# A banded convolution with its operands exchanged, and a transposing transfer in place of a bounce through DRAM

## The chip, the core and the metric

The kernel runs on one core of a Trainium2 chip. The metric is device time in microseconds; the kernel before takes 749.12 us (median of three runs, 748.72 to 749.59). The core has five engines that work side by side, each through its own list of instructions in order: PE (TensorE, the matrix unit; its weight loads are shown apart as PEld), ACT (ScalarE), DVE (VectorE), POOL (GpSimd) and SP (SyncE, which here only issues DMA transfers). They wait for each other through semaphores.

## The reference

```python
def _attn_ref(x, weight):                 # x (8, 4096, 192), weight (8 heads, 7 taps)
    ...
    w = softmax(weight, axis=-1)
    x_pad = zeros before the first token, 6 of them, per batch row
    x_unf = x_pad[:, idx, :].reshape(B, S, K, H, group)      # group = 24 channels per head
    out = np.einsum('hk,bskhg->bshg', w, x_unf)

def _moe_ref(x, w_in, w_out):             # 32768 tokens, 192 -> 2048 -> 192
    h = x @ w_in
    g = np.where(h > 0.0, h, np.exp(np.minimum(h, 0.0)) - 1.0)
    return (g @ w_out).astype(np.float32)
```

So each token's 24 channels of a head become a weighted sum of the last seven tokens' channels (a causal convolution, seven taps per head), and the result goes through two matrix products with an ELU between them.

## The kernel before

Tokens are handled in 32 super steps of 1024 (two groups of 512; `s` or `t` counts super steps). In a super step the 2048 hidden columns are cut into 16 blocks of 128, so there are 512 "pairs" `n = 16 s + q`. Pair `n` computes hidden block `q` for both groups. Its chain is:

1. PE, L706 (`H`): three pairs of matmuls, `w_in` stationary, `att` moving, 512 columns each. The two matmuls of a pair use the upper and the lower 64 rows of the array at the same time and write to two banks of PSUM.
2. ACT, L499: `E = exp(H)`, one instruction per group.
3. POOL, L410: clip `E` to [0, 1].
4. DVE, L561: `gT = max(E - 1, H)`, in fp16. This frees the slot of `H`.

PSUM has three slots for `H` in a ring; a pair takes the next one and waits until whoever held it before is done (`wait_slot`; for an earlier pair that is DVE's L561). The second product (L741, `ops`) takes `gT` as stationary and `w_out` as moving operand, 192 columns, again as pairs over both row halves. These matmuls fill the gaps between the pairs: the list `GAPS` says how many go after which pair. One half of a super step's output is 64 such pairs, spread over seven gaps. An entry is "turned" when its row halves write to exchanged banks; where a list goes from unturned to turned entries of the same accumulator, PE waits (`s_swap`) until its own earlier matmuls have ended. When the last entry of a half is done, ACT evacuates (L470, `osb`) and SP sends the rows out (L322).

The convolution of a coming super step is put in the same gaps, twice per super step (`CONV_AT`): after pair 2 and after pair 10, each in the middle of a gap of two lists (5 entries, then 6 turned ones). A convolution item `("c", m)` takes one slot of the ring. It works as follows (L661 to L687). `xg` holds windows of 128 tokens as rows; `Tr` holds for each head a band matrix of 128 rows with the softmaxed taps. The window's 24 channels of a head are stationary and 122 band columns move, so that the output has channels as rows and tokens as columns: 8 heads, 5 pieces, 40 matmuls, four of which run side by side in column groups of 32. ACT copies the result to `csb` (L479, one instruction of 1024 columns). SP writes it to DRAM (`conv_slots`, L773) and, when it has landed, reads it back in the order that `att` needs with three transfers (L334). In all a super step has two writes and six reads for this. In every super step the convolution after pair 2 is for group 1 of the next super step, and that after pair 10 for group 0 of the one after it.

POOL also issues the loads of `x` (L362, two per super step, after pairs 3 and 11, five and four windows), two super steps ahead. SP's list holds, in order, the bounce's transfers and the output's.

The first super step is convolved in another way (L648), and the next three convolutions (`EARLY_CONV`, after pairs 3, 6 and 10 of super step 0) write to `ops`, which is not yet in use; `warm_pair` puts matmuls on zeros between the first pairs. In the last super step there is no convolution left.

The order of PE, ACT and SP around a convolution is made by one list:

```python
for n in range(NP):
    s, i = divmod(n, NQ)
    slot_of_pair[n] = take_slot(("h", n))
    order.append(("h", n))
    gaps = list(rounds_at.get(n, ()))
    if len(gaps) == 2:
        order.append(("o", gaps.pop(0)))
    ...
    if s:
        for at, ahead, g in CONV_AT:
            if at == i and s + ahead < NS:
                conv_at(s + ahead, g)
    if gaps:
        order.append(("o", gaps[0]))
```

Of the kernel before, what the change touches and what calls it, by code (L numbers as in the profile page):

```python
# [12 lines left out]
P = 128  # L13
HP = 64
# [4 lines left out]
CPH = 24  # L19
SLOT = 32  # L20
CW = 122
ZW = 256
GS = 512
SUP = 2 * GS
PAD = KSIZE - 1
NWIN = 9
NXB = 2
# [7 lines left out]

CONV_AT = ((2, 1, 1), (10, 2, 0))
EARLY_CONV = {3: (1, 0), 6: (1, 1), 10: (2, 0)}
FREE_CONV = 3
QUAD = 4
XTW = 136  # L40
HALO = 2
XW = 5
X_AT = ((3, 1), (8, 0), (11, 2))

PIECES = (
    ((0, 0, CW, 0), (1, 0, CW, CW), (2, 0, CW, 2 * CW), (3, 0, CW, 3 * CW), (4, 0, 24, 4 * CW)),
    ((4, 24, 24, 0), (5, 0, CW, 24), (6, 0, CW, 24 + CW), (7, 0, CW, 24 + 2 * CW),
     (8, 0, CW, 24 + 3 * CW)),
)


def bass_lightweight_conv__then__act_elu_kernel(
# [35 lines left out]

    def conv_at(s, g):
        m = 2 * s + g - 2  # L90
        if m >= FREE_CONV:
            slot_of_conv[m] = take_slot(("c", m))
        order.append(("c", m))

# [37 lines left out]
# [7 lines that stand above are left out]
        if n in EARLY_CONV:  # L139
            conv_at(*EARLY_CONV[n])  # L140
        if s:
            for at, ahead, g in CONV_AT:
                if at == i and s + ahead < NS:
                    conv_at(s + ahead, g)
        if gaps:
            order.append(("o", gaps[0]))
# [36 lines left out]
    taps = nc.dram_tensor("conv_taps", (HEADS, ZW), BF16).ap()  # L183
    bounce = nc.dram_tensor("conv_slots", (2, 2, P, SUP), BF16).ap()

    with ExitStack() as stack:
        def sbuf(name, shape, dt):
            return stack.enter_context(nc.sbuf_tensor(name, shape, dt))
# [4 lines left out]
        def sema(name):  # L193
            return stack.enter_context(nc.semaphore(name))
# [12 lines left out]
        sel = sbuf("sel", [HEADS, P], BF16)  # L207
        xg = sbuf("xg", [P, NXB, NWIN, D], BF16)
        Tr = sbuf("Tr", [P, HEADS, CW], BF16)
        csb = sbuf("csb", [P, 4, 2, GS], BF16)  # L210
        att = sbuf("att", [P, 2, 3, GS], BF16)
        w_in = sbuf("w_in", [P, 3, FF], BF16)
# [16 lines left out]
        s_wp = sema("s_wp")  # L229
        s_wb = sema("s_wb")  # L230
        s_wc = sema("s_wc")
        s_id = sema("s_id")
# [21 lines left out]
        s_ce = sema("s_ce")  # L254
        s_dw = [sema(f"s_dw{i}") for i in range(4)]
        s_band = sema("s_band")
# [16 lines left out]

        NDMA_ATT = 6
        x_need, z_need = {}, {}
# [47 lines left out]

        def read_att(eng, W, s, g):

            m = 2 * s + g - 2
            W(s_dw[m % 4], 16 * (m // 4 + 1))
            for j in range(3):
                src = bass.AP(
                    tensor=bounce.tensor,  # L330
                    offset=(2 * P * (s % 2) + j) * SUP + GS * g,
                    ap=[[SLOT * SUP, HEADS], [3 * SUP, 8], [1, GS]],
                )
                eng.dma_start(  # L334
                    att[HP * g : HP * (g + 1), s % 2, j, :], src
                ).then_inc(s_att[s % 2], 16)

        @block.gpsimd
        def _gpsimd(g: bass.BassGpSimd):
            W = Waits(g)  # L340

            def load_x(s, part):
                b, t0 = s % NXB, s * SUP
                first = s % SPB == 0
                if part == 0 and not first:
                    return
                if part == 0:
                    W(s_x[b][0], x_need[s, 0])
                    g.memset(xg[0:PAD, b, 0, :], 0.0).then_inc(s_z)
                    return  # L350
                if s > NXB:
                    W(s_cv, 2 * (s - NXB))
                if part == 1:
                    w0, w1, row = 0, XW, t0 - PAD
                else:
                    w0, w1, row = XW, NWIN, t0 + SUP - P - CW * (NWIN - 1 - XW)
                src = bass.AP(
                    tensor=x_flat.tensor,
                    offset=row * D,
                    ap=[[D, P], [CW * D, w1 - w0], [1, D]],  # L360
                )
                g.dma_start(xg[:, b, w0:w1, :], src).then_inc(s_x[b][part - 1], 16)  # L362

# [56 lines left out]
        def _scalar(a):  # L420
# [15 lines left out]
            for j in (0, 2):  # L436
# [4 lines left out]
            a.activation(  # L441
                att[:, 0, 0, :].rearrange("p (r t) -> p r t", r=2),
                ops[:, :, 0 : GS // 2],
# [33 lines left out]

            def conv_evac(m, b0, b1):
                return a.activation(  # L479
                    csb[:, m % 4, b0:b1, :], conv_bank(m)[:, b0:b1, :], ACT.Copy  # L480
                )

            for item in order:
                if item[0] == "c":
                    m = item[1]
                    W(s_cv, m + 1)
                    W(s_dw[m % 4], 16 * (m // 4))
                    if m < FREE_CONV:
                        conv_evac(m, 0, 1)
                        late.append(m)  # L490
                    else:
                        conv_evac(m, 0, 2).then_inc(s_ce)
                elif item[0] == "h":
# [8 lines left out]
                    if late:  # L502
                        conv_evac(late.pop(), 1, 2).then_inc(s_ce)
                else:
# [4 lines left out]
        def _vector(v):  # L509
# [37 lines left out]
            v.tensor_copy(  # L547
                att[:, 0, 1, :].rearrange("p (r t) -> p r t", r=2),
                H[:, 2, :].rearrange("p (r t) -> p r t", r=2)[:, :, 0 : GS // 2],
# [3 lines left out]
                att[:, 0, 2, GS // 2 : GS], H[:, 0, GS : GS + GS // 2]  # L553
            ).then_inc(s_hd)
            for n in range(NP):
                s, q = divmod(n, NQ)
# [20 lines left out]
        def _tensor(pe):  # L577
# [83 lines left out]
            for x_, item in enumerate(order):  # L661
                if item[0] == "c":
                    m = item[1]
                    s, g = divmod(m + 2, 2)
                    if m == 0:
                        W(s_band, 32)
                    for part in range(g + 1):
                        W(s_x[s % NXB][part], x_need[s, part])
                    W(s_z, z_need[s])
                    if m < FREE_CONV:  # L670
                        conv_read(W, m - 1)
                    else:
                        wait_slot(slot_of_conv[m])
                    to = conv_bank(m)
                    for hb in range(2):
                        for (w, c0, nc_, o) in PIECES[g]:
                            for q in range(4):
                                h = 4 * hb + q
                                ins = pe.matmul(  # L679
                                    to[SLOT * q : SLOT * q + CPH, hb, o : o + nc_],  # L680
                                    xg[:, s % NXB, w, CPH * h : CPH * (h + 1)],
                                    Tr[:, h, CW - c0 - nc_ : CW - c0][:, ::-1],
                                    start=True,
                                    stop=True,
                                    tile_position=(0, SLOT * q),
                                )
                    ins.then_inc(s_cv)  # L687
                elif item[0] == "h":
# [10 lines left out]
                    else:  # L699
                        W(s_wc, 16)  # L700
                    W(s_att[s % 2], 16 * NDMA_ATT * ((s + 1) // 2))
                    k = slot_of_pair[n]
                    wait_slot(k)
                    for j in range(3):
                        for r in range(2):
                            ins = pe.matmul(  # L706
                                H[:, k % 3, GS * r : GS * (r + 1)],
                                w_in[HP * r : HP * (r + 1), j, FC * q : FC * (q + 1)],
                                att[HP * r : HP * (r + 1), s % 2, j, :],
                                start=(j == 0),  # L710
# [42 lines left out]
        def _sync(sy):  # L753
# [14 lines left out]
            for item in order:  # L768
                if item[0] == "c":
                    m = item[1]  # L770
                    s, g = divmod(m + 2, 2)
                    conv_read(W, m)
                    sy.dma_start(  # L773
                        bounce[s % 2, :, :, GS * g : GS * (g + 1)].rearrange("b p t -> p b t"),
                        csb[:, m % 4, :, :],
                    ).then_inc(s_dw[m % 4], 16)
                    if m == 1:
                        read_att(sy, W, s, 0)
                    if g == 1:
                        read_att(sy, W, s, g)  # L780
                elif item[0] == "h":
                    s, i = divmod(item[1], NQ)
                    if i == 1 and s >= 1 and s + 1 < NS:
                        W(s_h, NQ * s)
                        read_att(sy, W, s + 1, 0)
                elif item[0] == "o":
# [41 lines left out]
```

## Time and profile before

| what | value |
|---|---|
| median of three runs | 749.12 us |
| the profiled execution: its time, its span | 747.89 us, 746.2 us |
| POOL, ACT and DVE busy, share of the span | 89%, 87%, 85% |
| DVE L561, 1024 instructions, mean | 682 ns |
| POOL L410, 1024 instructions, mean | 615 ns |
| ACT L499, 1024 instructions of 512 columns, mean | 605 ns |
| ACT L479, 59 instructions of 1024 columns, mean | 1024 ns |
| ACT L470, 63 instructions of 768 columns, mean | 817 ns |
| SP's issue of one read of the bounce (L334), median | 582 ns |
| `conv_slots<-csb`, 256 KB, issue to landing, median | 2.5 us |
| `xg<-in_x_dram`, 240 KB and 192 KB, issue to landing, median | 5.2 us and 4.5 us |

The profile is of one execution; its times are in microseconds from the start of its span. In the views below a row of the timeline gives the start, the length, the engine, the line, the operation, what it writes and reads, how many instructions were merged, and in brackets the idle time before it and what ended it. Matmuls overlap: the end of one is modelled, and the distance between the starts of two groups is the time that PE needs for the first.

### The profile page before, as it was taken

What the parts mean: (1) busy time and instruction counts of PE and PEld (TensorE: products, weight loads), DVE (VectorE), ACT (ScalarE), POOL (GpSimd) and SP (SyncE); (2) the same over time, 40 slices, a digit from 0 to 9 for tenths busy, and PEclk for the clock granted to TensorE, in tenths of its full rate; (3) what the DMA queues carried; (4) which work ended last, traced back from release to release, by engine and by line L of the source; (5) the groups of instructions that cost most, each with busy time, mean ns of one, the idle gap of its engine ahead of it and who ended that gap; (6) DMA issues with size and microseconds to landing.
All of it is one profiled execution on the core that took longest, in us unless ns stands there. A gap on an engine that the chain in (4) does not pass through costs nothing.

```text
span 746.2 us, 32212 instructions
## 1 busy us (share of the span) xinstructions
PE 735.6 (99%) x13850; PEld 517.2 (69%) x13850; DVE 637.9 (85%) x1041; ACT 647.0 (87%) x1165; POOL 660.8 (89%) x1107
## 2 busy tenths in 40 slices
PE   7899999999999999999999999999999999999998
PEld 4567777777777677776677777776776776777666
DVE  5988988888889889889889888888898898888894
ACT  6888888898888898888888888988888888888884
POOL 8888989989989989889989899899898898899883
PEclk9999999999999999999999999999999999999999
DMA  9654453453543543444434435535435435345112
GB/s 174 134 107 89 101 107 84 104 106 79 112 90 88 113 97 88 93 101 101 107 88 103 98 90 107 107 73 118 85 92 110 94 93 115 77 103 106 60 44 65
DMA packets 107038, 72.79 MB, mean 98 GB/s; under 512 B 44552, under 2 KB 106640, under 8 KB 106896
## 3 DMA queue, kind: packets, MB, share of 16 engines
q1 hardware_dynamic: 66384, 54.47, 24.0%
q0 software_dynamic: 40224, 15.78, 19.7%
q8 instruction: 108, 1.77, 1.0%
q10 hardware_dynamic: 288, 0.49, 0.2%
q14 instruction: 34, 0.28, 0.1%
HBM read 44.78 MB, written 41.42 MB: 116 GB/s over the span
## 4 chain that ended last, share of the span: by engine, by line
PE 96%; DVE 1%; ACT 1%; DMA 1%; issue 0%; POOL 0%; SPq 0%
PE ops L741 46%; PE H L706 45%; PE H L679 5%; DVE gT L561 1%; PE H L741 1%; DMA xf<-in_x_dram 1%; ACT E L499 0%; POOL E L410 0%; PE H L648 0%; PE ops L648 0%; ACT csb L479 0%; ACT xT L438 0%; PE H L616 0%; DVE xh L536 0%; SPq L755 0%
## 5 line engine op out<-in xcount | busy, mean ns | idle before, releaser
L561 DVE SCALAR_TENSOR_TENSOR gT<-E,H 128x512 f16<-128x512 f32 x1024 | 632.8, 682 | 92.8 <-POOL E L410 86.4
L410 POOL TENSOR_SCALAR E<-E 128x512 f32<-128x512 f32 x1024 | 604.3, 615 | 72.9 <-ACT E L499 68.0
L499 ACT ACTIVATE E<-H 128x512 f32<-128x512 f32 x1024 | 546.0, 605 | 83.3 <-PE H L706 74.6
L741 PEld LDWEIGHTS ops<-w_out,gT 64*128 64x128 f16 x8064 | 345.3, 94 | 106.6 <-ACT osb L470 10.8
L741 PE MATMUL ops<-w_out,gT 64*128 64x192 f16 x8064 | 416.8, 243 | 0.3
L706 PE MATMUL H<-att,w_in 64*128 64x512 bf16 x3072 | 407.7, 377 | 2.5 <-DVE gT L561 1.9
L706 PEld LDWEIGHTS H<-att,w_in 64*128 64x128 bf16 x3072 | 134.1, 94 | 99.2 <-issue 5.8
L479 ACT ACTIVATE csb<-H 128x1024 bf16<-128x1024 f32 x59 | 60.4, 1024 | 0.0
L470 ACT ACTIVATE osb<-ops 128x768 f32<-128x768 f32 x63 | 51.5, 817 | 6.2 <-PE ops L741 6.2
L362 POOL DMA_DIRECT2D xg<-in_x_dram x62 | 52.2, 842 | 0.4 <-issue 0.4
L679 PE MATMUL H<-Tr,xg 128*24 128x122 bf16 (+1 forms) x2360 | 38.6, 209 | 0.0
L679 PEld LDWEIGHTS H<-Tr,xg 128*24 128x24 bf16 x2360 | 29.6, 92 | 9.3 <-issue 9.3
L741 PE MATMUL H<-w_out,gT 64*128 64x192 f16 x128 | 5.9, 243 | 0.0
L572 DVE COPY osb<-H 128x192 f32<-128x192 f32 x1 | 0.4, 358 | 6.3 <-PE H L741 6.3
L741 PEld LDWEIGHTS H<-w_out,gT 64*128 64x128 f16 x128 | 5.3, 94 | 0.0
L592 PE MATMUL ops<-zw 128*128 128x512 bf16 x9 | 4.0, 631 | 1.2 <-DVE zw L511 1.2
L367 POOL DMA_DIRECT2D w_in<-in_moe_w_in_dram x7 | 4.6, 657 | 0.3 <-DMA wh<-in_weight_dram 0.3
L479 ACT ACTIVATE csb<-ops 128x512 bf16<-128x512 f32 x6 | 3.7, 623 | 0.3 <-PE ops L679 0.3
L597 PE MATMUL ops<-zw 64*128 64x512 bf16 x12 | 2.3, 380 | 1.7 <-ACT csb L479 1.7
L592 PEld LDWEIGHTS ops<-zw 128*128 128x128 bf16 x9 | 1.2, 142 | 3.2 <-issue 1.9
L679 PEld LDWEIGHTS ops<-Tr,xg 128*24 128x24 bf16 x120 | 1.6, 92 | 2.0 <-issue 2.0
L597 PEld LDWEIGHTS ops<-zw 64*128 64x128 bf16 x12 | 0.6, 94 | 3.1 <-ACT csb L479 2.7
(47 smaller groups left out, 26.1 us busy)
## 6 DMA issues: line engine op xcount, KB each, us to landing
out_dram<-osb SPq DMA_DIRECT2D x126, 192.0 KB, 2.7
conv_slots<-csb SPq DMA_DIRECT2D x62, 256.0 KB, 2.5
att<-conv_slots SPq DMA_DIRECT2D x186, 64.0 KB
xg<-in_x_dram POOLq DMA_DIRECT2D x31, 240.0 KB, 5.2
xg<-in_x_dram POOLq DMA_DIRECT2D x31, 192.0 KB, 4.5
w_out<-in_moe_w_out_dram POOLq DMA_DIRECT2D x1, 768.0 KB, 14.8
w_in<-in_moe_w_in_dram POOLq DMA_DIRECT2D x2, 240.0 KB, 8.0
xf<-in_x_dram ACTq DMA_DIRECT2D x1, 384.0 KB, 3.3
```

Source lines behind the costliest of these rows:

```text
L362: g.dma_start(xg[:, b, w0:w1, :], src).then_inc(s_x[b][part - 1], 16)
L367: g.dma_start(w_in[HP * r : HP * (r + 1), :, c0:c1], moe_w_in.rearrange("(p j) f -> p j f", j=3)[:, :, c0:c1],).then_inc(s_w[k], 16)
L410: g.tensor_scalar(out=E[:, n % NE, u, :], in0=E[:, n % NE, u, :], scalar1=1.0, scalar2=0.0, op0=ALU.min, op1=ALU.max,).then_inc(s_clp)
L470: a.activation(osb[:, b, :, :, :].rearrange("p g k d -> p g (k d)"), ops[:, :, 0 : 2 * D], ACT.Copy,).then_inc(s_oev)
L479: return a.activation(csb[:, m % 4, b0:b1, :], conv_bank(m)[:, b0:b1, :], ACT.Copy)
L499: a.activation(E[:, n % NE, u, :], H[:, k, GS * u : GS * (u + 1)], ACT.Exp).then_inc(s_exp)
L561: v.scalar_tensor_tensor(out=gT[:, s % NG3, q, u, :], in0=E[:, n % NE, u, :], scalar=1.0, in1=H[:, slot_of_pair[n] % 3, GS * u : GS * (u + ...
L592: pe.matmul(ops[:, 0, :], zw[:, 0:P], zw[:], start=True, stop=True)
L597: pe.matmul(ops[:, r, :], zw[HP * r : HP * (r + 1), 0:P], zw[HP * r : HP * (r + 1), :], start=True, stop=True, tile_position=(HP * r, 0),)
L679: ins = pe.matmul(to[SLOT * q : SLOT * q + CPH, hb, o : o + nc_], xg[:, s % NXB, w, CPH * h : CPH * (h + 1)], Tr[:, h, CW - c0 - nc_ : CW ...
L706: ins = pe.matmul(H[:, k % 3, GS * r : GS * (r + 1)], w_in[HP * r : HP * (r + 1), j, FC * q : FC * (q + 1)], att[HP * r : HP * (r + 1), s ...
L741: ins = pe.matmul(acc[:, g, d0 : d0 + D], gT[HP * rt : HP * (rt + 1), t % NG3, q, g, t0 : t0 + P], w_out[HP * rt : HP * (rt + 1), q, :], s ...
```

## The change

The convolution exchanges its operands: the band is stationary and the tokens' channels move, so the output has tokens as rows and channels as columns. Windows are 112 tokens apart, ten to a super step (five per group). An item is now four heads for all ten windows (the `u`-th four heads), not one group for all heads. A matmul has 64 rows of the band (half of the 128 token rows) and 240 moving columns (2 groups x 5 windows x 24 channels); the two row halves of one head must be added, and they are, in PSUM: first pass with the upper half on bank 0's head and the lower half on bank 1's, second pass with the banks exchanged. So an item is 4 matmuls, then four entries of the gap's second list, then 4 matmuls, then the rest of the list. The second pass waits for the end of the first (`s_cs`). ACT evacuates with two instructions of 480 columns, whose write order puts the 64 rows of each group side by side for three channel parts. Both convolutions of a super step are for the next one, and when the second has been evacuated SP issues one transposing transfer (112 rows x 1920 columns of 2 bytes, 430,080 bytes) from `csb` to `att`. The DRAM bounce is gone. The band is reversed once at the start into `Tm` by DVE, ahead of its main loop. The second load of `x` has five windows as well; for the last super step the last window is loaded by an extra transfer. Two early convolutions remain (after pairs 3 and 7), each of which waits for both loads of `x`.

```diff
-CW = 122
+CW = 128
+TOK = 112
+WPG = 5
+HB = 2
+BN = HB * CPH * 2 * WPG
+GAP_SPLIT = 4
...
-CONV_AT = ((2, 1, 1), (10, 2, 0))
-EARLY_CONV = {3: (1, 0), 6: (1, 1), 10: (2, 0)}
-FREE_CONV = 3
+CONV_AT = ((2, 1, 0), (10, 1, 1))
+EARLY_CONV = {3: (1, 0), 7: (1, 1)}
+FREE_CONV = 2
...
+        order.append(("c", m, 0))
+        between = []
+        if gap:
+            between, gap[:] = gap[:GAP_SPLIT], gap[GAP_SPLIT:]
+        if between:
+            order.append(("o", between))
+        order.append(("c", m, 1))
...
-        def read_att(eng, W, s, g):
...
+        def turn_att(eng, s):
+            eng.dma_start_transpose(
+                out=att[:, s % 2, :, :].rearrange("p j (w t) -> p (j w) t", t=TOK),
+                in_=csb[0:TOK, s % 2, :],
+            ).then_inc(s_att[s % 2], 16)
...
-            def conv_evac(m, b0, b1):
+            def conv_evac(m, b):
+                s, u = m // 2 + 1, m % 2
+                h0 = 4 * u + HB * b
                 return a.activation(
-                    csb[:, m % 4, b0:b1, :], conv_bank(m)[:, b0:b1, :], ACT.Copy
+                    csb[:, s % 2, :].rearrange(
+                        "p (j v h i) -> p h j v i", j=3, v=2 * WPG, h=HEADS
+                    )[:, h0 : h0 + HB],
+                    conv_bank(m)[:, b, 0:BN].rearrange(
+                        "p (h v i j) -> p h j v i", h=HB, v=2 * WPG, j=3
+                    ),
+                    ACT.Copy,
                 )
...
+            W(s_band, 32)
+            v.tensor_copy(Tm[:], Tr[:, :, ::-1]).then_inc(s_tm)
             for n in range(NP):
...
-                    for hb in range(2):
-                        for (w, c0, nc_, o) in PIECES[g]:
-                            for q in range(4):
-                                h = 4 * hb + q
-                                ins = pe.matmul(
-                                    to[SLOT * q : SLOT * q + CPH, hb, o : o + nc_],
-                                    xg[:, s % NXB, w, CPH * h : CPH * (h + 1)],
-                                    Tr[:, h, CW - c0 - nc_ : CW - c0][:, ::-1],
...
+                    for hh in range(HB):
+                        for rt in range(2):
+                            b = rt ^ turned
+                            h = 4 * u + HB * b + hh
+                            n1 = BN // HB
+                            ins = pe.matmul(
+                                to[:, b, n1 * hh : n1 * (hh + 1)],
+                                Tm[HP * rt : HP * (rt + 1), h, :],
+                                xg[HP * rt : HP * (rt + 1), s % NXB, :, :].rearrange(
+                                    "p (g w) d -> p w g d", g=2
+                                )[:, :, :, CPH * h : CPH * (h + 1)],
+                                start=(hh == 0 and not turned),
+                                stop=(hh == HB - 1 and turned == 1),
+                                tile_position=(HP * rt, 0),
+                            )
...
-                    m = item[1]
-                    s, g = divmod(m + 2, 2)
-                    conv_read(W, m)
-                    sy.dma_start(
-                        bounce[s % 2, :, :, GS * g : GS * (g + 1)].rearrange("b p t -> p b t"),
-                        csb[:, m % 4, :, :],
-                    ).then_inc(s_dw[m % 4], 16)
...
+                    _, m, turned = item
+                    s = m // 2 + 1
+                    if turned and m % 2:
+                        conv_read(W, m)
+                        W(s_h, NQ * (s - 1))
+                        turn_att(sy, s)
```

## The prediction

> **What bounds the kernel now.** I read the page's busy shares and its chain of waits first. PE is busy throughout, at full clock, and the chain stays on PE: 46% second product, 45% first, 5% convolution.
>
> ```profile
> PE 735.6 (99%) x13850; PEld 517.2 (69%) x13850; DVE 637.9 (85%) x1041; ACT 647.0 (87%) x1165; POOL 660.8 (89%) x1107
> ...
> PEclk9999999999999999999999999999999999999999
> ...
> PE 96%; DVE 1%; ACT 1%; DMA 1%; issue 0%; POOL 0%; SPq 0%
> PE ops L741 46%; PE H L706 45%; PE H L679 5%; DVE gT L561 1%; PE H L741 1%; DMA xf<-in_x_dram 1%; ACT E L499 0%; POOL E L410 0%; PE H L648 0%; PE ops L648 0%; ACT csb L479 0%; ACT xT L438 0%; PE H L616 0%; DVE xh L536 0%; SPq L755 0%
> ```
>
> But 99% holds only because ends of matmuls are modelled. The timeline of one steady half super step, from the convolution after pair 10 to the one after pair 2, shows the rest:
>
> ```profile
> 409.82 0.57 PE L741 MATMUL ops<-w_out,gT 64*128 64x192 f16 x10
> 410.32 0.65 PE L679 MATMUL H<-Tr,xg 128*24 128x122 bf16 x40
> 410.90 0.67 PE L741 MATMUL ops<-w_out,gT 64*128 64x192 f16 x12
> 411.04 1.02 ACT L479 ACTIVATE csb<-H 128x1024 bf16<-128x1024 f32 x1
> 411.41 0.81 PE L706 MATMUL H<-att,w_in 64*128 64x512 bf16 x6
> 411.84 0.79 POOL L362 DMA_DIRECT2D xg<-in_x_dram  x1
> 412.26 1.09 ACT L499 ACTIVATE E<-H 128x512 f32<-128x512 f32 x2 [0.20 <-PE H L706]
> 413.23 0.82 ACT L470 ACTIVATE osb<-ops 128x768 f32<-128x768 f32 x1
> 413.92 3.10 ACT L499 ACTIVATE E<-H 128x512 f32<-128x512 f32 x6
> 415.08 0.81 PE L706 MATMUL H<-att,w_in 64*128 64x512 bf16 x6
> 415.27 8.72 DVE L561 SCALAR_TENSOR_TENSOR gT<-E,H 128x512 f16<-128x512 f32 x14 [0.39 <-POOL E L410]
> 415.73 0.99 PE L741 MATMUL ops<-w_out,gT 64*128 64x192 f16 x20
> 416.61 0.82 PE L706 MATMUL H<-att,w_in 64*128 64x512 bf16 x6
> 417.90 0.82 PE L706 MATMUL H<-att,w_in 64*128 64x512 bf16 x6
> 421.68 0.66 PE L679 MATMUL H<-Tr,xg 128*24 128x24 bf16 x40
> 422.78 0.81 PE L706 MATMUL H<-att,w_in 64*128 64x512 bf16 x6
> ```
>
> PE's prices are distances between starts: a group of three pairs of 512 columns 0.65 (415.08 to 415.73), so 217 ns a pair; ten pairs of 192 columns 0.82 (414.26 to 415.08 in the same view), so 82 ns a pair; a convolution 0.58 plus 0.09 on entry (409.82 + 5 x 0.082 = 410.23, it starts at 410.32). The half lasts 11.36; the next convolution is at 433.01, so two take 22.69, 11.34 on average.
>
> A loop through all engines is as tight as PE. After the convolution ACT copies it, then does pair 11's exponentials at 412.26, then `osb` at 413.23, then pair 12's at 413.92. POOL and DVE follow, and from 415.27 DVE runs 14 instructions without a gap, one starting 0.60 to 0.62 after the other (two alone take 1.28, so 1.28 - 0.68 = 0.60; (8.72 - 0.68) / 13 = 0.62). PE needs a slot of H back from DVE: pair 15 at 416.61 stands 0.06 behind its place (415.73 + 0.82 = 416.55), pair 0 at 417.90 some 0.13 behind. So what delays ACT's row at 412.26 delays DVE's run, and through pair 0 the next half: that row is what I cost the change at.
>
> **The same half without a convolution.** Super step 31 has none; weight loads there show the period and PE's wait for itself at the change from unturned to turned entries:
>
> ```profile
> 705.35 0.44 PEld L741 LDWEIGHTS ops<-w_out,gT 64*128 64x128 f16 x12 [0.32 <-PE ops L741]
> ...
> 716.26 0.44 PEld L741 LDWEIGHTS ops<-w_out,gT 64*128 64x128 f16 x12 [0.30 <-PE ops L741]
> ```
>
> A period of 10.91, so a convolution costs the kernel 0.43 a half. The self wait costs PE 0.26: eleven pairs take 1.17 (726.50 to 727.67 in the last stretch of the timeline) where 11 x 0.082 is 0.91.
>
> **The change, part by part,** for a half; there are 60 with a convolution in the loop (59 before).
>
> *PE.* 40 matmuls go, 8 come. No row has 240 columns; between 82 ns at 192 and 217 at 512 a straight line gives 102 ns a pair, four pairs 0.41 for 0.58: 0.17 less, if the row halves overlap as in L706 and L741, which have the same shape. Should they run one after the other, 0.82: 0.24 more. I take 0.17, since the form is theirs. The self waits: between the first list and its turned one now lies pass one, 0.20, and the entry, 0.09; together 0.29, more than the 0.26. Between the passes lie four entries, 0.33, more than 0.26 too. I take 0, bounds 0 and 0.10 each (a wait that keeps its weight loads from being prefetched, as the entry's 0.09 now).
>
> *ACT, the part that decides.* Before, pair 11's exponentials start 1.94 after the convolution (410.32 to 412.26), and PE ended that wait; ACT itself was done at about 411.95. After: pass one 0.20, four entries 0.33, start of the last pair 0.10, its length 0.27 (a row of L648 with 256 columns has 268 ns), 0.07 until ACT starts (410.97 to 411.04): 0.97, and with 0.05 for two waits 1.02. Then two copies of 480 columns. ACT's rows give 605 ns at 512 and 1024 ns at 1024, 0.82 ns a column, so 579 ns; behind one another instructions of 512 columns start about 0.48 apart, so 0.45 here: 0.90. Sum 1.92 against 1.94. ACT becomes the one that ends this wait, at the same place, and PE's 0.17 goes into waiting. That is the forecast: 0 a half, with 0.02 of PE's small waits on top. Bounds: the copies read every third column and write runs of eight, which no row does. At the price of DVE's copy of 512 columns from PSUM, 693 ns, each is 0.11 longer: 0.22 a half. Below: if they cost nothing more than fits, pair 11 comes 0.17 earlier, but DVE's run lets only about 0.07 through. Pair 3 needs DVE's twelfth result of the run: 415.27 + 11 x 0.61 + 0.68 = 422.66, and 0.05 for the semaphore (the weight load of pair 15 starts that long after its result); it stands at 422.78.
>
> *The transposing transfer.* It takes the place of a path with 12 us to spare: the bounce's last read of a super step is issued at 403.16 (SP in the same view) and its reader starts at 417.90. The new one can be issued when the second copy ends: 410.32 + 1.02 + 0.45 + 0.58 = 412.4, and pair 0 reads at 417.90, with 0.1 for the semaphore: 5.4 us. What is past that, PE waits in full, 30 times; behind the waiting pair stand all of PE's lists, and ACT, POOL and DVE behind them. The trace of before has no such transfer. Its fixed part: 256 KB land in 2.4 to 2.9, of which the bytes take 0.8 at q1's rate (54.47 MB in 24.0% of 746.2 us, 304 GB/s), so 1.6. Its moving part, from below: 430 KB at that rate, 1.4, in all 3.0. By packets of a 256-byte row, 112 x 15 = 1680 of them: the nearest row is the band's load, 244 bytes a packet (window 6.5 to 10.5: q1 901 packets, 0.22 MB, 31.4%, so 22 ns each), 2.3 on 16 engines, in all 3.9; at q1's mean of 43 ns 4.5, in all 6.1. From above: if each 32-byte run at the destination is a packet, 128 x 105 = 13,440 at 22 ns, 18.5, in all 20. It shares the engines with the load of x issued at 411.84, whose 640 packets (128 x 5) take 2.3 at q0's mean (19.7% of 746.2 us on 16 engines over 40224 packets, 58 ns): half of that still ahead adds 1.1. I take the row of like size, 3.9 + 1.1 = 5.0: it lands, with 0.4 to spare.
>
> The Trainium skill speaks on both sides here, and no run has yet shown it. "DMA: Bandwidth & Descriptors", Latency and other measured facts, gives a transposing transfer 261 GB/s with a non-contiguous middle dimension: 1.6 us for these bytes, an estimate, and the transfer would be hidden with more room than I give it. "VectorE: DVE Perf Modes", The three transpose paths, gives 1309 ns for one 128x128 block through the crossbar: if the 15 blocks went one after the other that is 19.6 us, an estimate from that page, and some 430 us on the sum.
>
> *SP, POOL, DVE.* 62 writes and 186 reads leave SP; none was waited for by PE in the list of waits, so they give nothing. Behind SP's new wait stand the output's transfers of the half, which wait for `osb` at 414.05 anyway. POOL's second load has five windows, 0.89 for 0.79; POOL idles 0.32 after it (412.63 to 412.95), so nothing; uncovered it would be 31 x 0.10 = 3. DVE's reversal, 1024 columns, between 0.56 (768 columns, L536) and 1.4 (twice L545's 0.69): it falls into DVE's 2.30 of idle time before its first L561 at 13.08, and the band's load is over by 10.5. Uncovered, 1.
>
> *Start and end.* The first convolution now waits for the second load of x (issued 7.28, 8.8 to landing, 16.1; before it started at 15.17): 1.0 later. One early convolution with its two copies of 0.6 is gone, which gives about as much back: 0, give or take 1. One more convolution in the loop: 0.43.
>
> **Sum.** 60 x 0.02 + 0.43 = 1.6 on the profiled 747.89 (span 746.2 and 1.7 around it), so 749.5; the median stands 1.23 above the profiled time: 751.
>
> **The rivals.**
> *The transfer lands late* (slower). For it: the margin is 0.4, the mean packet price alone gives 6.1 without sharing. Against: the packet of like size costs half. At 6.1 plus 0.4 of sharing it is 1.1 late, 30 x 1.1 = 33: 784. It decides from 5.4 us on, 30 us for each us; at the far bound, 20, some 1190.
> *PE's saving gets through* (faster). If the copies cost less than 0.45, up to DVE's 0.07: 747.89 + 0.43 - 60 x 0.07 + 1.23 = 745; with DVE's run out of the way too, 60 x 0.17, 739. For it: the forecast's tie at 1.92 is made of six terms. Against: two instructions for one, and DVE's own run.
> *The copies or passes are dearer* (slower): 0.22 a half, 13 us: 764. This is also the case in which the two passes do not overlap, 0.24 a half.
>
> **How the numbers follow.** Forecast 0.42 (its own range 747 to 756, by waits of 0.10 a half), late transfer 0.30, saving through 0.20, dearer copies or passes 0.08. A run tells about 0.2%, 1.5 us, from no change. Faster: 0.20 and 0.04 of the forecast's spread, 0.24. Same: 0.13 of the forecast's and 0.02 of the saving's neighbourhood, 0.15. Slower: the rest, 0.61. The range goes from 743 to 790: below it the saving past 0.10 a half, about 0.05, above it the late transfer past 6.7, about 0.15.
>
> **What would show it.** Transfer: the weight load of the pair that begins a super step waits for the DMA, and every second half is longer. Hidden: halves alike near 11.36. ACT's tie: the idle time before the exponentials after a convolution ended by nothing of PE's, csb rows near 580 ns. PE: eight matmuls of the convolution within 0.75, four entries among them. It is wrong if the transfer takes over 5.4 us, or csb rows are far from 580.

## The result, and the profile after

The changed kernel takes 786.1 us (median of four runs, 778.04 to 787.04); the kernel before, run beside it, 748.92 (748.72 to 749.59). The ratio is 1.0471, 95% interval 1.0401 to 1.0541: slower. The profiled execution took 785.51 us with a span of 783.6, 37.4 more than before's 746.2.

Four views of the profile after: the busy shares and the chain of waits (with what each line has of it), a group of instructions each for the pair, the copy and the reversal, and the median times from issue to landing.

```profile
PE 737.9 (94%) x11870; PEld 503.6 (64%) x11870; DVE 638.5 (81%) x1042; ACT 646.0 (82%) x1224; POOL 663.0 (85%) x1108
...
PE 67%; DMA 25%; ACT 3%; issue 2%; DVE 1%; POOL 1%; ACTq 0%; DVEq 0%
PE H L732 32%; PE ops L767 31%; DMA att<-csb 24%; PE H L700 3%; ACT csb L482 2%; DMA Tr<-conv_taps 1%; DVE gT L576 1%; PE H L767 1%; ACT E L512 1%; POOL E L411 0%; DMA conv_taps<-zt 0%; ACT L424 0%; POOL xg L363 0%; POOL xg L354 0%; DVE Tm L569 0%
...
L732 PE MATMUL H<-att,w_in 64*128 64x512 bf16 x3072 | 411.5, 381 | 38.6 <-DMA att<-csb 32.5
...
L482 ACT ACTIVATE csb<-H 128x480 bf16<-128x480 f32 x120 | 61.9, 568 | 7.9 <-PE H L700 0.4
...
L569 DVE COPY Tm<-Tr 128x1024 bf16<-128x1024 bf16 x1 | 0.4, 426 | 5.3 <-DMA Tr<-conv_taps 5.3
...
xg<-in_x_dram POOLq DMA_DIRECT2D x61, 240.0 KB, 5.4
...
att<-csb SPq DMA_TRANSPOSE x31, 6.3
```

The chain was 96% PE before and is 67% PE now: 24% of it is the transposing transfer (`att<-csb`), which takes 6.3 us at the median, and PE sat idle 32.5 us until it landed. How often is in the list of waits (total, times, longest). The third and the fourth row are smaller new waits. Weight loads of a pair wait for DVE to free a slot, 3 times before, 45 times now; 4.6 of the 16.4 us are one wait at the start, 28 of the 45 stand at pair 3 and 8 at pair 11, the first pairs behind a convolution. And weight loads of turned entries wait for PE's own earlier matmuls, 3 times before, 35 times now:

```profile
PEld H L732 <- DMA att<-csb: 38.8, 28, 3.1
PE H L732 <- DMA att<-csb: 32.5, 28, 2.9
PEld H L732 <- DVE gT L576: 16.4, 45, 4.6
PEld ops L767 <- PE ops L767: 5.6, 35, 0.3
```

28 of the 31 transfers are waited for. The timeline of a typical half, from the convolution after pair 10 to the one after pair 2, shows one of these waits:

```profile
455.86 0.37 PE L700 MATMUL H<-xg,Tm 64*128 64x240 bf16 x4
456.12 0.50 PE L767 MATMUL ops<-w_out,gT 64*128 64x192 f16 x8
...
456.46 0.37 PE L700 MATMUL H<-xg,Tm 64*128 64x240 bf16 x4
...
456.87 1.03 ACT L482 ACTIVATE csb<-H 128x480 bf16<-128x480 f32 x2
...
457.46 0.89 POOL L363 DMA_DIRECT2D xg<-in_x_dram  x1
...
457.85 1.08 ACT L512 ACTIVATE E<-H 128x512 f32<-128x512 f32 x2
457.92 1.59 SPq L328 DMA_TRANSPOSE att<-csb  x1
...
462.86 0.66 PE L767 MATMUL ops<-w_out,gT 64*128 64x192 f16 x12
...
464.27 0.82 PE L732 MATMUL H<-att,w_in 64*128 64x512 bf16 x6 [0.75 <-DMA att<-csb]
...
467.96 0.38 PE L700 MATMUL H<-xg,Tm 64*128 64x240 bf16 x4
```

Pair 0 could start at 462.86 + 0.66 = 463.52; it starts at 464.27. SP issued the transfer at 457.92, so 5.60 us were there, and 6.3 were needed. POOL had issued a load of `x` 0.46 ahead of it. The half lasts 12.10, before 11.36. The median of the 28 waits is 0.83; eight of them are 1.4 to 2.9 us long.

Some halves are longer still. Seven of the transfers took 7.4 to 8.4 us, and after three waits in the loop the granted clock of PE fell to half for 3.4 us, at 250.8, 581.9 and 609.2. The first of these, in the view by stretches (length, busy time of PE, PEld, DVE, ACT and POOL with instructions in brackets, granted clock, share of the DMA engines' time, GB/s):

```profile
246.00:250.00 4.00, 1.96 (x36) 1.23 (x30) 4.00 (x7) 2.11 (x5) 3.33 (x6) 1.00 1.01 205
250.00:253.00 3.00, 2.57 (x22) 1.60 (x24) 0.19 (x2) 1.08 (x2) 0.73 (x2) 0.64 0.02 6
253.00:257.00 4.00, 4.00 (x64) 2.92 (x62) 2.65 (x5) 2.38 (x5) 2.39 (x5) 0.85 0.00 0
```

PE waited 2.47 us there, and the half took 15.43. By the typical half it should have been 12.10 - 0.75 + 2.47 = 13.82: the low clock cost 1.6. The other two (waits of 2.05 and 2.12, halves of 14.93 and 15.07) give 1.5 and 1.6 in the same way. Over the whole run the granted clock was 0.997 in the fastest of the four (778.04) and 0.991 in the others.

So the 37.4 us are, by the starts of the convolutions in both traces:

| stretch | before | after | difference |
|---|---|---|---|
| span's start to the first convolution of the loop | 36.08 | 39.08 | +3.0 |
| 29 halves with the transfer (pair 10 to pair 2) | 329.3 | 365.6 | +36.3 |
| 29 halves without (pair 2 to pair 10) | 328.5 | 326.2 | -2.3 |
| the rest, with one half more that has a convolution | | | +0.4 |

The halves without the transfer are 0.08 shorter (11.25 for 11.33), so the exchanged operands do save something. The others sum to 328.1 in the first experiment below, where no transfer is waited for; the 37.5 above that are PE's 32.5 of waiting, 4.7 of low clock, and 0.3 whose cause isn't shown.

The +3.0 at the start is in two rows of the timeline:

```profile
16.14 0.43 DVE L569 COPY Tm<-Tr 128x1024 bf16<-128x1024 bf16 x1 [5.31 <-DMA Tr<-conv_taps]
...
17.82 0.82 PE L732 MATMUL H<-att,w_in 64*128 64x512 bf16 x6 [4.12 <-DVE gT L576]
```

DVE waited 5.31 us for the band before it could reverse it, all of its `gT` stood behind that wait, and PE behind them: pair 3 starts at 17.82, before at 14.42. A stretch of half clock follows PE's wait of 4.12 here too, from 18.71 to 22.12.

### The profile page after: what moved, and what is told of

Its sections match the earlier page's. It is cut to its first block, busy times and chain, and to the rows that moved or that the text cites. A ratio compares the mean times of both kernels' runs of the same rounds, so it can differ in the third digit from the quotient of the medians.

```text
span 783.6 us, 28045 instructions
## 1 busy us (share of the span) xinstructions
PE 737.9 (94%) x11870; PEld 503.6 (64%) x11870; DVE 638.5 (81%) x1042; ACT 646.0 (82%) x1224; POOL 663.0 (85%) x1108
## 4 chain that ended last, share of the span: by engine, by line
PE 67%; DMA 25%; ACT 3%; issue 2%; DVE 1%; POOL 1%; ACTq 0%; DVEq 0%
PE H L732 32%; PE ops L767 31%; DMA att<-csb 24%; PE H L700 3%; ACT csb L482 2%; DMA Tr<-conv_taps 1%; DVE gT L576 1%; PE H L767 1%; ACT E L512 1%; POOL E L411 0%; DMA conv_taps<-zt 0%; ACT L424 0%; POOL xg L363 0%; POOL xg L354 0%; DVE Tm L569 0%
## 5 line engine op out<-in xcount | busy, mean ns | idle before, releaser
L732 PE MATMUL H<-att,w_in 64*128 64x512 bf16 x3072 | 411.5, 381 | 38.6 <-DMA att<-csb 32.5
L767 PE MATMUL ops<-w_out,gT 64*128 64x192 f16 x8064 | 427.6, 244 | 0.2
L732 PEld LDWEIGHTS H<-att,w_in 64*128 64x128 bf16 x3072 | 129.7, 95 | 150.8 <-DMA att<-csb 38.8
L482 ACT ACTIVATE csb<-H 128x480 bf16<-128x480 f32 x120 | 61.9, 568 | 7.9 <-PE H L700 0.4
L363 POOL DMA_DIRECT2D xg<-in_x_dram x62 | 55.4, 893 | 0.1
L700 PE MATMUL H<-xg,Tm 64*128 64x240 bf16 x480 | 44.6, 263 | 0.2 <-DVE gT L576 0.2
L700 PEld LDWEIGHTS H<-xg,Tm 64*128 64x128 bf16 x480 | 20.5, 94 | 1.4 <-issue 0.4
L482 ACT ACTIVATE csb<-ops 128x480 bf16<-128x480 f32 x4 | 2.4, 602 | 0.0
```

The lines of the kernel that those rows point to most:

```text
L363: g.dma_start(xg[:, b, v0 : v0 + whole, :], src).then_inc(s_x[b][part - 1], 16)
L482: return a.activation(csb[:, s % 2, :].rearrange("p (j v h i) -> p h j v i", j=3, v=2 * WPG, h=HEADS)[:, h0 : h0 + HB], conv_bank(m)[:, b, ...
L700: ins = pe.matmul(to[:, b, n1 * hh : n1 * (hh + 1)], Tm[HP * rt : HP * (rt + 1), h, :], xg[HP * rt : HP * (rt + 1), s % NXB, :, :].rearran ...
L732: ins = pe.matmul(H[:, k % 3, GS * r : GS * (r + 1)], w_in[HP * r : HP * (r + 1), j, FC * q : FC * (q + 1)], att[HP * r : HP * (r + 1), s ...
L767: ins = pe.matmul(acc[:, g, d0 : d0 + D], gT[HP * rt : HP * (rt + 1), t % NG3, q, g, t0 : t0 + P], w_out[HP * rt : HP * (rt + 1), q, :], s ...
```

## The experiments

The theory under test is that the load of `x` makes the transfer late, and that its reader's deadline makes that cost something. The times quoted from the traces are of one profiled execution. Ratios are to the kernel before, run on the same chip at the same time.

**1. The load of `x` taken away from beside the transfer.** Both loads are issued after pair 3, half a super step earlier; the transfer, the output's transfers behind it and its deadline stay.

```diff
-X_AT = ((3, 1), (8, 0), (11, 2))
+X_AT = ((3, 1), (3, 2), (8, 0))
```

> The changed kernel with both loads of x issued after pair 3, so that none stands beside the transposing transfer. Sharing theory: the transfer needs about 3.5 us alone (the first and the last one in the changed kernel's trace, which have no load of x beside them, took 3.56 and 3.45) and the load adds 2.8; without it, about 3.5 to 4 us to landing, under the 5.4 that are there, so no wait of PE for it, and the half from pair 10 to pair 2 falls from a median of 12.15 to about 11.25. POOL's second issue after pair 3 costs about 0.7 of DVE's run in the other half, 11.25 to at most 12. Time 750 to 770. Rival, the transfer itself is slow in the loop (its 105 tiles, or the output's transfers behind it): still 6 us, half still 12.15, time 785 or more.

762.67 us (761.74 to 763.45), ratio 1.0191 (1.0176 to 1.0205). Times from issue to landing (minimum, median, maximum), then the half with the transfer and the start of the next, in the timeline:

```profile
DMA to landing us min/median/max: 3.4/3.4/5.3
```

```profile
420.10 0.37 PE L700 MATMUL H<-xg,Tm 64*128 64x240 bf16 x4
...
422.16 1.45 SPq L328 DMA_TRANSPOSE att<-csb  x1
...
427.69 0.82 PE L732 MATMUL H<-att,w_in 64*128 64x512 bf16 x6
...
431.38 0.38 PE L700 MATMUL H<-xg,Tm 64*128 64x240 bf16 x4
...
432.98 1.77 POOL L363 DMA_DIRECT2D xg<-in_x_dram  x2
...
435.44 3.08 DVE L576 SCALAR_TENSOR_TENSOR gT<-E,H 128x512 f16<-128x512 f32 x5 [1.67 <-POOL E L411]
...
436.78 0.82 PE L732 MATMUL H<-att,w_in 64*128 64x512 bf16 x6 [0.45 <-DVE gT L576]
```

The transfer falls from 6.3 to 3.4 us, pair 0 at 427.69 has no idle time before it, and the half is 11.28. The output's transfers still stand behind it on SP's queue, so they were not what made it slow; the load of `x` was. The price shows in the other half: POOL issues two loads in a row, 1.77 us, its clips come late, DVE idles 1.67 and PE waits 0.45 for a slot, at pair 6 in 28 super steps. That half is 11.71 for 11.25, and 30 times 0.46 is the 13.8 us by which its sum rises.

**2. The transfer kept beside a load, with a later deadline.** The convolutions go back to the places of the kernel before: after pair 2 the second item of the next super step, after pair 10 the first of the one after. The transfer is issued after pair 2 and read 13 pairs later. `x` is loaded one half super step earlier to match.

```diff
-CONV_AT = ((2, 1, 0), (10, 1, 1))
-EARLY_CONV = {3: (1, 0), 7: (1, 1)}
-FREE_CONV = 2
+CONV_AT = ((2, 1, 1), (10, 2, 0))
+EARLY_CONV = {3: (1, 0), 7: (1, 1), 11: (2, 0)}
+FREE_CONV = 3
...
-X_AT = ((3, 1), (8, 0), (11, 2))
+X_AT = ((3, 2, 2), (8, 2, 0), (11, 3, 1))
```

> The changed kernel with the convolutions placed as before the change (after pair 2 for the second four heads of the next super step, after pair 10 for the first four heads of the one after it), and the loads of x one half earlier to match. The transposing transfer is then issued after pair 2 and has some 20 us. Lateness theory: no wait of PE for it, whatever it takes (about 6.3 us beside a load of x); both halves at 11.25, time 749 + 3 (start) - 59 x 0.09 = 747, and no stretch at half clock but that of the start. Rival, the new form of the convolution costs by itself (copies, two passes): halves of 11.4 or more, time over 752.

748.16 us (745.48 to 750.39, 12 runs), ratio 0.9992 (0.9978 to 1.0006). The times to landing are as bad as in the changed kernel:

```profile
DMA to landing us min/median/max: 3.5/6.4/8.2
```

Nobody waits for them, the granted clock stays full through the loop, and the halves are 11.24 and 11.27. So the size of transfer that kept PE waiting 32.5 us in the changed kernel costs PE nothing here; what differs is the deadline. No gain over before could be told from these runs. The profiled execution is the fastest of the twelve (745.48) and the only one with a granted clock of 1.000; the other eleven had 0.995 to 0.999, and where they lost it is not on record.

**3. The reversal of the band moved behind DVE's first pairs.** The two early convolutions, which need the reversed band, move back with it; everything else is the changed kernel.

```diff
-            W(s_band, 32)
-            v.tensor_copy(Tm[:], Tr[:, :, ::-1]).then_inc(s_tm)
             for n in range(NP):
+                if n == 3:
+                    W(s_band, 32)
+                    v.tensor_copy(Tm[:], Tr[:, :, ::-1]).then_inc(s_tm)
...
-EARLY_CONV = {3: (1, 0), 7: (1, 1)}
+EARLY_CONV = {5: (1, 0), 9: (1, 1)}
```

> The changed kernel with DVE's reversal of the band after pair 2's results in place of ahead of its loop, and the two early convolutions after pairs 5 and 9. Theory of the start: DVE waited 5.3 us for the band's load, which put the first convolution of the loop at 39.08 in place of 36.08; here it is at 36 to 37, and the time is 2 to 3 us under the changed kernel's, 783. Rival, the start is bound by the loads of x and w_in: first convolution of the loop still at 39, time 786.

776.51 us (774.06 to 781.56), ratio 1.0386 (1.0354 to 1.0417). From the first pair to the first convolution of the loop it takes 24.82 us instead of 28.15: 3.3 less. That convolution stands at 37.59 all the same, past the expected 36 to 37 (39.08 in the changed kernel), since the first pair comes at 12.77 here and at 10.93 there.

The median fell by 9.6, more than the 2 to 3 expected. The profiled execution is 7.2 shorter than that of the changed kernel (778.29 for 785.51): 1.5 of it lies ahead of this convolution, 5.6 in the 29 halves with the transfer, which sum to 360.0 instead of 365.6, with five of the transfers over 7 us instead of seven. The edit does not touch these halves, and what made them shorter is not shown. The wait that the edit removes varies as well: in experiment 2, where the reversal stands as in the changed kernel, DVE waits only 1.6 us for the band and reverses it at 12.7.

**4. Both edits.** The later deadline and the later reversal, `EARLY_CONV = {5: (1, 0), 8: (1, 1), 11: (2, 0)}`.

> Both of the former together: early placement of the convolutions and the late reversal. If both theories hold: halves of 11.25, first convolution of the loop at 36 to 37, time 743 to 745, under the kernel before by 4 to 6. If only the placement matters, 747; if neither, over 752.

746.17 us (745.06 to 746.95, 8 runs), ratio 0.9968 (0.9959 to 0.9978): 0.3% faster than the kernel before, and faster than with either edit alone. The expected 743 to 745 was not reached. Timeline of the half from the convolution after pair 2 to the one after pair 10, and a row of the list of waits:

```profile
421.49 0.39 PE L701 MATMUL H<-xg,Tm 64*128 64x240 bf16 x4
...
422.49 1.03 ACT L482 ACTIVATE csb<-H 128x480 bf16<-128x480 f32 x2
422.61 0.33 PEld L733 LDWEIGHTS H<-att,w_in 64*128 64x128 bf16 x6 [0.22 <-DVE gT L577]
...
423.47 1.08 ACT L512 ACTIVATE E<-H 128x512 f32<-128x512 f32 x2
423.55 1.60 SPq L328 DMA_TRANSPOSE att<-csb  x1
...
432.79 0.38 PE L701 MATMUL H<-xg,Tm 64*128 64x240 bf16 x4
```

```profile
PEld H L733 <- DVE gT L577: 12.8, 44, 1.3
```

The weight load of pair 3 waits 0.22 for DVE, which must free the slot that pair 1 held; in all there are 44 such waits, 12.8 us, 31 of them at pair 3 and 8 at pair 11. By the trace PE's saving is stopped there; no run makes DVE faster to test it. The 58 distances between convolutions of the loop sum to 653.6 instead of before's 657.8, 4.2 less; the start is 2.2 later (38.27 for 36.08). Most of that is the first pair, at 12.55 (38.27 less the 25.72 that follow) where before's is at 10.88 (36.08 less 25.20). That is not the edit's doing: the same sixteen matmuls ahead of it are slower in this execution (experiment 7, alike up to there, has the first pair at 10.84). First the kernel before, then this one:

```profile
7.50 1.06 PE L648 MATMUL ops<-xT,Dg 64*128 64x256 bf16 x16 [0.33 <-ACT xT L438]
7.81 1.89 PE L664 MATMUL ops<-xT,Dg 64*128 64x256 bf16 x16
```

The first record of full clock begins at 5.72 in before's trace and at 10.67 in this one. All ten profiled executions go this way: where that record begins at 4.1 to 5.7, the first pair stands at 10.7 to 11.2; where it begins at 10.0 to 10.7, at 12.2 to 12.6. In experiment 3 it begins at 4.5, but half clock follows from 7.92 to 11.33, and the first pair stands at 12.77.

**5. No entries between the two passes.** On kernel 4, `GAP_SPLIT = 0` instead of 4: the second pass now follows the first directly and meets `s_cs`.

> The kernel with early placement and late reversal, but the two passes of a convolution back to back: no entries of the second product between them. PE's wait for its own first pass then comes out: 0.26 as measured before the change, so PE needs about 0.25 more per convolution. If DVE's run sets the half (pair 3 and pair 11 stand 0.06 behind their slot, with 0.14 of PE's time unused before them), about 0.14 of it is absorbed and halves go from 11.25 to about 11.35, 6 us in all, time 752. If PE sets the half: 11.5, time 760. If the passes need no wait: 746.

749.29 us (748.68 to 750.1), ratio 1.0006 (0.9997 to 1.0015), 3.1 more than kernel 4. Timeline of one convolution:

```profile
423.56 0.84 PE L701 MATMUL H<-xg,Tm 64*128 64x240 bf16 x8
424.01 0.11 PEld L701 LDWEIGHTS H<-xg,Tm 64*128 64x128 bf16 x4 [0.34 <-PE H L701]
...
424.23 0.66 PE L768 MATMUL ops<-w_out,gT 64*128 64x192 f16 x12
```

```profile
PEld H L701 <- PE H L701: 20.5, 59, 0.4
PEld H L733 <- DVE gT L577: 4.2, 6, 1.3
```

PE's wait for itself is real: 20.5 us in 59 weight loads. The next group starts 0.67 after the convolution, where two passes of 0.20 need 0.41, so PE loses 0.26 of the 0.34. Of this only 0.04 to 0.09 reaches the half (11.31 and 11.33), and in exchange the waits for DVE's slot fall from 12.8 us in 44 to 4.2 in 6: most of one wait hides in the other. The four entries are worth their place.

**6. One of the two copies left out.** On kernel 4; `csb` is set to zero once.

```diff
-                    conv_evac(m, 0)
...
-                        conv_evac(m, 1).then_inc(s_ce)
+                        conv_evac(m, 0).then_inc(s_ce)
```

> The kernel with early placement and late reversal, with ACT's second copy of each convolution left out, so half of the heads' convolution is not evacuated and the output is not the reference's; csb is set to zero once at the start (up to 2 us there). If ACT's two copies set the half (my tie at 1.92), 0.45 of ACT's time goes and halves fall from 11.25 to 11.1 or less, 9 us or more in all. If DVE's run sets it, as the 0.06 between DVE's result and pair 3's start says, halves stay within 0.03 of 11.25.

745.2 us (744.46 to 745.68), ratio 0.9951 (0.9936 to 0.9966). The timeline behind the convolution after pair 2, and then, from the convolution on, at the place of the forecast's tie, after pair 10:

```profile
420.83 0.57 ACT L483 ACTIVATE csb<-H 128x480 bf16<-128x480 f32 x1
420.94 0.33 PEld L736 LDWEIGHTS H<-att,w_in 64*128 64x128 bf16 x6 [0.22 <-DVE gT L580]
...
421.81 1.09 ACT L514 ACTIVATE E<-H 128x512 f32<-128x512 f32 x2 [0.41 <-PE H L736]
```

```profile
408.61 0.37 PE L704 MATMUL H<-xg,Tm 64*128 64x240 bf16 x4
...
410.51 1.08 ACT L514 ACTIVATE E<-H 128x512 f32<-128x512 f32 x2 [0.33 <-PE H L736]
```

ACT is free 0.41 us earlier (0.33 after pair 10) and then waits for PE. After pair 2 the exponentials start 1.99 after the convolution (419.82), as in kernel 4 (423.47 - 421.49 = 1.98); after pair 10 they start 1.90 after it (408.61 to 410.51), in kernel 4 1.93 (410.25 to 412.18). The halves are 11.27 and 11.215, at most 0.03 less. ACT's copies do not set the half; the wait of pair 3 for DVE's slot stands ahead of them, unchanged at 0.22.

**7. Earlier early convolutions.** On kernel 4, `EARLY_CONV = {4: (1, 0), 7: (1, 1), 10: (2, 0)}`.

> The kernel with early placement and late reversal, with the three early convolutions after pairs 4, 7 and 10 in place of 5, 8 and 11. The first entries of the second product waited 0.89 for the copies of the third early convolution; one pair earlier this is gone: about 1 us less, 745. If the second load of x or the band is later than that in most executions, the same or up to 1 us more.

746.28 us (745.19 to 746.73), ratio 0.9962 (0.9949 to 0.9974): the same as kernel 4. The gain expected did not show. In the profiled execution the first early convolution, behind pair 4 at 15.57, comes too early for its load of `x` and for the reversed band (its weight load waits 2.3 us for DVE), the other case that the expectation names:

```profile
18.23 1.03 PE L701 MATMUL ops<-xg,Tm 64*128 64x240 bf16 x8 [1.83 <-DMA xg<-in_x_dram]
```

**8. The load beside the transfer cut to two windows of five.** On the changed kernel; the other three are loaded after pair 3.

```diff
-X_AT = ((3, 1), (8, 0), (11, 2))
+X_AT = ((3, 1), (3, 2), (8, 0), (11, 3))
```

> The changed kernel with three of the second load's five windows issued after pair 3 and only two beside the transposing transfer. Sharing theory: the transfer is slowed by what is left of the load, 3.45 + 2.85 x 2/5 = 4.6 us to landing, under the 5.4 that are there, no wait for it, half from pair 10 to pair 2 at 11.28. If any load ahead of it holds it up by a fixed time, still about 6 and halves of 12. The other half carries an extra issue on POOL, 11.6 to 11.8, as with both loads after pair 3.

760.75 us in one run.

```profile
DMA to landing us min/median/max: 3.5/4.4/6.2
```

With no window, two and five beside it, the transfer takes 3.4, 4.4 and 6.3 at the median. At 4.4 it fits. Eleven of the 31 take 4.9 to 6.2, and the list of waits has 4.4 us of weight loads in 7 waits for the transfer, where the changed kernel has 38.8 in 28. The other half pays for POOL's second issue, as in experiment 1: 11.61.

## Why the prediction was right or wrong

The side and the range held, and what came was the rival called late transfer (784 us, 786.1 measured). The likeliest case, a transfer that lands hidden at 751, was wrong, and that the rival's figure came within 2.1 us is in part luck, as shown below.

**The step that failed** is the term of sharing: "half of that still ahead adds 1.1". The transfer without a load beside it takes 3.4 to 3.5, so the load adds 2.9, not 1.1. The trace's packets show how. Alone, the first packet of a transfer starts 1.2 us after its issue and the last ends at 3.0 at the median; behind the load the first starts at 2.1 to 2.9 and the last ends at 5.8 at the median. So it both starts later and runs longer: about the whole time of the load issued before it is added, which I had priced myself at 2.3 us of the sixteen engines, and then counted half, without a reason. The kernel before had a sign against that half: a load of 240 KB took 5.2 us there from issue to landing, and the transfer was to be issued some 0.5 us behind it. With the whole 2.3, the prediction's own 3.9 gives 6.2, past the 5.4 by 0.8, and the median wait is 0.83; but this comes out because 3.9 is 0.5 too much and 2.3 is 0.6 too little. Experiments 1 and 8 show the dose (0, 2 and 5 windows), experiment 2 that the time of the transfer costs something only against its deadline.

**What stood.** The issue came 2.06 us after the convolution (455.86 to 457.92; predicted 2.08) and 5.60 were there (predicted 5.4). The price of the kind, 256-byte packets at 22 ns and 1.6 fixed, gave 3.9 for 3.4 to 3.5 measured; of the ends 3.0, 3.9, 6.1 and 20, the first is as near. An estimate from the Trainium skill, "DMA: Bandwidth & Descriptors", Latency and other measured facts (261 GB/s, 1.6 us, with the same fixed part 3.2) is somewhat nearer. The 1309 ns of "VectorE: DVE Perf Modes", The three transpose paths, do not add up over the 15 blocks: all of them land in 3.4 us. The rival's total of waits held as well, 32.5 for 33, though not in its parts: it had the transfer alone at 6.1 and 0.4 of sharing, where 3.4 and 2.9 were measured, and 1.1 in each of 30 halves, where 0.83 is the median and eight of the 28 waits are 1.4 or longer. It lacked the low clock (4.7 us) and the start (3.0), and it took nothing off for what the convolution saves (2.3 in the halves without the transfer, 1.2 in the others); that these partly cancel is the luck.

**ACT's tie.** The copies take 568 ns (predicted 579) and follow each other 0.46 apart (predicted 0.45), the eight matmuls 263 ns each (268): these sizes were right. So was the place: the exponentials of pair 11 start 1.92 after the convolution at the median (predicted 1.92; 1.99 in the half shown), with no idle time before them. But the tie was not what decides. Experiment 6 removes half of ACT's work there and they start at 1.90, where I had them at 1.77 without a tie, and PE ends that wait. The first pair behind a convolution is itself held, by the slot that DVE frees: most often pair 3. The saving that gets through is 0.06 to 0.12 a half (11.36 and 11.33 before; 11.28 and 11.25 in experiment 1 and the changed kernel, 11.24 and 11.27 in experiments 2 and 4). This is the limit that the rival "PE's saving gets through" named, DVE's run at pair 3, with 0.07 a half. In the halves without the transfer it showed already in the changed kernel.

**PE's waits for itself** were put at 0, with a bound of 0.10 each. Between the passes there is none in the changed kernel's list of waits. Behind pass one a little is left: the turned entries' weight loads wait (35 times, 5.6 us), and the entries start 0.26 after pass one (455.86 to 456.12), where pass two takes 0.20 (456.46 to 456.66). The eight matmuls and the entries between take 0.80, where 0.75 was named as the sign. Without the entries between, the weight load waits 0.34 (experiment 5).

**POOL's second load, and SP**: 0.89 for 0.79, hidden, as said. That POOL has no room for a further issue (experiments 1 and 8) was not part of the prediction.

**The start.** "The band's load is over by 10.5" was wrong: I took the end of one window (6.5 to 10.5) for the end of the load. The window has 901 packets of the queue; the load has 1024, and the last ends at 11.98 in before's trace, at 15.61 in the changed kernel's, where DVE could not start before 16.14. Uncovered I had put the reversal at 1; the wait for the band before it was not priced at all. It cost 3.0 in the profiled execution, and experiment 3 gets 3.3 back.

**Left open**: why about a quarter of the transfers behind a load take 7.1 to 8.4, where most take 6.0 to 6.5 (experiments 2 and 4 have them as well, unharmed; in experiment 1, with no load beside them, five of 31 take 4.1 to 5.3 instead of 3.4); why the band's load ends at 12.29 in experiment 2 and at 15.61 in the changed kernel; and how much of the scatter of experiment 2's runs is the clock's. These were not tried.

## What to carry to other kernels

Price a new transfer as the whole of what was issued just ahead of it plus its own time alone (here 2.9 and 3.4 us), and hold that against the reader's deadline. Where the margin is less than one such load, move the reader away first: here half a period more was worth 38 us (experiment 2), and moving the neighbouring load 23 (experiment 1).

A saving on an engine that others follow closely can stop at the next slot which has to come free: the 0.17 a half that PE was forecast to save became about 0.1. Before you tune the engine that seems tied, take its work away once (experiment 6) and see whether the period moves.

## What the runs showed of the hardware that I had not expected

- A transposing transfer from SBUF to SBUF of 430,080 bytes (112 x 1920 of 2 bytes) lands 3.4 to 3.5 us after its issue; with 240 KB of a load issued 0.46 us ahead of it 6.3, with 96 KB 4.4.
- Half clock after short waits: in the changed kernel's loop three of the 28 waits, of 2.05, 2.12 and 2.47 us, were followed by 3.4 us of half the granted clock; one of 2.90 was not (the pair at 200.75). The Trainium skill, "TensorE: Matmul & The Clock Gate", What's actually happening, has the clock fall after at least one idle window of about 3.4 us, and the window free-running. The length of the slow stretch agrees; the waits here were shorter than a window, and their length does not tell which of them hit.
- What tells it here is how much of a wait falls into one step of a fixed grid. Ahead of its last microsecond this trace has four slow stretches; they begin at 18.71, 250.81, 581.91 and 609.22, which is 68, 97 and 8 steps of 3.413 us apart. In the four steps just ahead of them PE is idle for 2.53, 2.47, 1.94 and 2.12 us (by the modelled ends of matmuls); in no other step since its first full clock is it idle for more than 1.90. The wait of 2.90 lies across two steps, 1.77 and 1.13. Experiments 1, 7 and 8 follow this once each at the start (2.07, 2.06, 2.27), experiment 3 in three steps (2.06, 1.99, 2.09), but not in one of 2.01 nor in its slow stretch at 7.92 (1.29), so no sharp bound is shown.
- ACT's copy that reads every third column of PSUM and writes runs of eight takes 568 ns for 480 columns, no more than its rows of 512 contiguous columns (605 to 609 ns) let one expect.
